# The second half's first LayerNorm, made on x passed in turned layout, with row statistics spread through DRAM

## The chip, the cores and the metric

The kernel runs on one core of one Trainium2 chip. Five engines work side by side, each executing its own queue in order: TensorE (PE, with its weight loads listed apart as PEld), VectorE (DVE), ScalarE (ACT), GpSimd (POOL) and SyncE (SP), which here only issues transfers; 16 DMA engines move the data. The metric is the device time of one execution in microseconds (us); less is better. A change of 0.2% is 3.5 us.

## The reference

One transformer block in float32, S = 2048 rows of width D = 512, with six modulation vectors from a condition c:

```python
mod = (_silu(c) @ w_mod).reshape(c.shape[0], 6, 1, -1)
sa, ca, ga, sb, cb, gb = (mod[:, 0], ..., mod[:, 5])
h = _layernorm(x, axis=-1) * (1 + ca) + sa
x = x + ga * attention(h)      # 32 query heads, 8 key/value heads, the last 512 keys
h = _layernorm(x, axis=-1) * (1 + cb) + sb
x = x + gb * ((gelu(h @ w_gate) * (h @ w_up)) @ w_down)
```

LayerNorm here is (x - mean) / sqrt(var + 1e-5) along a row. The change concerns the first LayerNorm, for rows 1024 to 2047 alone.

## The kernel before

**Numbers.** Float32 operands are split into two float16 parts, high and low, and every product is made of three float16 matmuls (`mm3`, line 83; the matmul's own line is 87). From group 3 on the projections use a seven-product scheme on 2 x 2 blocks, which needs sums and differences of blocks of h ("combos", t1 to t4).

**The main loop.** Attention is worked in 512 steps. A step t makes the scores of 128 query rows of one head against the 512 keys (`scores`, "ps", in one of two PSUM banks), then on VectorE the row maximum (`peak`, "nm", line 974), on ScalarE the exponential (`expo`, "ee", line 983), and two and three steps later the float16 parts of the probabilities (`high` on ScalarE, line 995; `low` on VectorE, line 1000). SP then turns these by a transposing transfer ("pt"). Four steps are a unit, one head on 512 query rows; 16 steps are a group (two heads, two row blocks). Steps 0 to 255 treat rows 0 to 1023, steps 256 to 511 rows 1024 to 2047; the first half's h is generation 0, the second half's generation 1. Between the scores TensorE works off a list, three items of three matmuls a step: projections ("qa", "qb", "qc"), probabilities times values ("po"), output projections ("py").

**Order.** All is written out by hand: each engine executes its instructions in the order in which the Python code issues them, step by step. Within a step the scores come first, then the maximum, `low`, the exponential, `high`, the list's items, the loads that are due, and last the work hung on the step as `("w", t)`. VectorE's work hung on step t therefore stands ahead of the maximum of step t + 1.

**Loads.** Float32 tiles go through the pool "raw" of five buffers. `sched(pos, (load, steps), ...)` names the steps at which a tile is used; a load is issued three steps ahead of its first use, or later where a slot, counted in rotation, is not free by the last use of the tile five loads earlier, but no later than the first use's step. SP issues in order, so a transfer that waits for an engine holds those behind it.

**GpSimd's other work** in each group of 16 steps, for the first half: the scale of the next weights (`w_spread`, one step ahead of the group, powers in tiles "lw", "lt"), the five parts of a weight set (`set_steps`, at 2, 3, 4, 6 and 8 steps into a group), a split of the keys at 9, of the values at 6 in every second, and four "wo" tiles for every second group (`parts`, line 640): at 6 and 4 steps before and 10 and 12 steps into it, but for the group of step 192 at 6, 4, 3 and 2 steps before it.

**The changed part.** `plan_gen(1, ...)` normalizes rows 1024 to 2047 ahead of time, in eight tiles of 128 rows, one every 16 steps from step 78 to step 190. For a tile first used at step t, `ln_tile` (lines 465 to 516) does: at t the statistics on VectorE (lines 378 to 382) and the power -1/2 on GpSimd (line 388); at t + 3 the norm on VectorE (line 486); at t + 5 four 128 x 128 float32 transposes on TensorE into a PSUM bank "pln" (line 491); at t + 6 and t + 7 the affine on ScalarE, four pieces of 128 x 128 (line 499), and a store of h to DRAM ("hs"); at t + 8 and t + 9 the high parts on ScalarE (line 511) and the low parts on GpSimd (line 513), for the blocks b11 and b21 (all columns of the first 512 rows) and b22 (the last 256 columns of the other 512). From step 201 on, and again from 234, `combos` reloads four columns' blocks from DRAM and makes t1 to t4 (lines 365, 369, 565). The same `ln_tile` serves a second LayerNorm elsewhere (generation 2), which stays.

Of the kernel before, what the change touches and what calls it, by code (L numbers as in the profile page):

```python
# [21 lines left out]
KT = D // P  # L22
NF = F // P
NT = S // P
QB = 512
QT = QB // P
EPS = 1e-5
# [31 lines left out]


@with_exitstack
def block_kernel(ctx: ExitStack, tc: tile.TileContext, x, kT, v, wq, wo, wg, wu, wd, cT, wc, wm, out):
    nc = tc.nc

    const = ctx.enter_context(tc.tile_pool(name="const", bufs=1))
    pool = ctx.enter_context(tc.tile_pool(name="pool", bufs=2))
    small = ctx.enter_context(tc.tile_pool(name="small", bufs=4))
    dram = ctx.enter_context(tc.tile_pool(name="dram", bufs=1, space=bass.MemoryType.DRAM))
# [5 lines left out]
    def raw(name):  # L74
        return pool.tile([P, 512], F32, tag="raw", name=name, bufs=NRAW)
# [4 lines left out]
    def bank(tag, name, bufs):  # L80
        return psum.tile([P, 512], F32, tag=tag, name=name, bufs=bufs)
# [9 lines left out]
    def dma(out_, in_):  # L91
        moved[0] += 1
        nc.sync.dma_start(out_, in_)
# [5 lines left out]
    def rows_of(t, i):  # L99
        return t[i * P:(i + 1) * P, :]  # L100
# [8 lines left out]
    nhalf = const.tile([P, 1], F32, name="nhalf")  # L109
# [19 lines left out]
    cols = const.tile([P, 6, KT], F32, name="cols")  # L129
# [105 lines left out]
    def pool_ts(out, src, a, b=1.0, op0=ALU.mult, op1=ALU.mult):  # L235
        nc.gpsimd.tensor_scalar(out, src, a, b, op0=op0, op1=op1)
# [136 lines left out]
    def ln_cols(key):  # L373
        return (1, 0) if key == "a" else (4, 3)

    def ln_stat(a, st, act=False):
        bn = small.tile([P, 6], F32, name="bn")
        nc.vector.bn_stats(bn, a)
        st["mv"] = small.tile([P, 2], F32, name="mv")
        nc.vector.bn_aggr(st["mv"], bn)  # L380
        st["rs"] = small.tile([P, 1], F32, name="rs")
        nc.vector.tensor_scalar(st["rs"], st["mv"][:, 1:2], EPS, None, op0=ALU.add)
        if act:
            st["nm"] = small.tile([P, 1], F32, name="nmean")
            nc.vector.tensor_scalar(st["nm"], st["mv"][:, 0:1], -1.0, None, op0=ALU.mult)

    def ln_power(st):
        nc.gpsimd.tensor_tensor(st["rs"], st["rs"], nhalf, op=ALU.pow)
# [78 lines left out]
    def ln_tile(gen, i, src):  # L467
        jsc, jsh = ln_cols("a" if gen < 2 else "f")
        qb, i = divmod(i % (2 * QT), QT)
        st = {}  # L470

        def load():
            if gen == 2:
                st["x"] = src()
            else:
                st["x"] = raw("xs")
                dma(st["x"], src())

        def stat():
            ln_stat(st["x"], st)  # L480
            ln_power(st)

        def norm():
            if gen == 2:
                return pool_ts(st["x"], st["x"], st["mv"][:, 0:1], st["rs"], ALU.subtract, ALU.mult)
            nc.vector.tensor_scalar(st["x"], st["x"], st["mv"][:, 0:1], st["rs"], op0=ALU.subtract, op1=ALU.mult)

        def turn():
            st["ps"] = bank("acc", "pln", NACC)
            for dt in range(KT):  # L490
                nc.tensor.transpose(st["ps"][:, dt * P:(dt + 1) * P], st["x"][:, dt * P:(dt + 1) * P], ident)

        def affine(dts):
            if 0 in dts:
                st["f"] = raw("hf") if gen == 2 else tmp("hf")
            f = st["f"]
            for dt in dts:
                sl = slice(dt * P, (dt + 1) * P)
                nc.scalar.activation(f[:, sl], st["ps"][:, sl], AF.Identity,
                                     scale=cols[:, jsc, dt:dt + 1], bias=cols[:, jsh, dt:dt + 1])  # L500
            if KT - 1 in dts:
                dma(spilled(gen, qb)[:, :, i * P:(i + 1) * P], f.rearrange("p (k q) -> p k q", k=KT))

        def parts(act):
            o = slice(i * P, (i + 1) * P)
            f = st["f"].rearrange("p (k q) -> p k q", k=KT)
            for h, name in enumerate(("b11", "b21") if qb == 0 else (None, "b22")):
                if name:
                    t, src = block(gen, name), f[:, 2 * h:2 * h + 2, :]
                    if act:  # L510
                        nc.scalar.activation(t[:, 0:2, o], src, AF.Copy)
                    else:
                        nc.gpsimd.tensor_tensor(t[:, 2:4, o], src, t[:, 0:2, o], op=ALU.subtract)

        more = [lambda: parts(True), lambda: parts(False)]
        return load, [stat, norm, turn, lambda: affine((0, 1)), lambda: affine((2, 3))] + more
# [82 lines left out]
    def sched(pos, ld, *more, kind="raw", ahead=AHEAD):  # L599
        loads.append(((pos,) + more, ld, kind, ahead))  # L600
# [121 lines left out]
    def at(key, *fns):  # L722
        later.setdefault(key, []).extend(fns)
# [442 lines left out]
    def sched_combos(gen, p, base):  # L1166
        for k, (load, steps) in enumerate(combos(gen, p, nc.gpsimd if gen or p == 0 else nc.vector, False, 0 if gen else 1 if p else 2, 0 if gen or p else 5)):
            if gen == 0 and (p == 0 or k > 1):
                at(base + ((0, 0, 0, 2)[k] if p else (-10, -2, -1, -9)[k]), load)
                for off, fn in steps:  # L1170
                    at(("w", base + off), fn)
            else:
                sched(base + steps[0][0], (load, [fn for _, fn in steps]), *[base + off for off, _ in steps[1:]])
# [1 line left out]
    for p in range(2):  # L1175
        sched_combos(0, p, CB[p])

    def plan_gen(gen, t_ln, t_cb, dcb, src):
        for i in range(2 * QT):
            t = t_ln[i]  # L1180
            load, steps = ln_tile(gen, i, lambda i=i: src(i))
            sched(t, (load, steps[:3]), t + 3, t + 5)
            for off, fn in zip((6, 7, 8, 9), steps[3:]):
                at(("w", t + off), fn)
        for p in range(2):
            sched_combos(gen, p, t_cb + dcb * p)

    plan_gen(1, [78 + 16 * i for i in range(8)], 201, 33, lambda i: rows_of(x, 2 * QT + i))
    for p in range(2):
        sched_combos(2, p, 478 + 10 * p)  # L1190

# [10 lines left out]
    for g in range(NG):  # L1202
        half, pr = divmod(g, NPR)
        t0 = 16 * g
# [404 lines left out]
    assert not later, list(later)  # L1609


_LAYOUT = ["x", "kT", "v", "wq", "wo", "wg", "wu", "wd", "cT", "wc", "wm"]


# [29 lines left out]
```

## Time and profile before

| what | value |
|---|---|
| median of 3 runs | 1746.63 us (1746.54 to 1746.77) |
| profiled execution, its time | 1747.24 us |
| its span | 1745.3 us |
| matmul busy, share of the span | 1723.9 us, 99% |
| VectorE, ScalarE, GpSimd busy | 79%, 70%, 52% |
| granted TensorE clock, mean | 1.00 |

The span is the part of the execution that the profile covers, from first to last instruction. A row of a timeline gives start and duration in us, engine, line, operation, output and inputs by the program's names, the shape and a count; in square brackets stands the idle time of the engine just before it and what ended that. A row of a group gives, under a tile's name, the least, median and largest duration in ns.

### The profile page before, as it was taken

To read this page: it belongs to the slowest core of one execution; us is meant where nothing else is said; L and a number is where in the kernel's file an instruction comes from. 1 tells how busy PE (TensorE), PEld (TensorE's weight loads), DVE (VectorE), ACT (ScalarE), POOL (GpSimd) and SP (SyncE) were. 2 spreads that over 40 slices of the span, in tenths; PEclk is the share of its full clock that TensorE was granted. 3 is DMA by queue.
4 is the path that set the end of the run, shared out by engine and by line. 5 is a ranking of instruction groups with operands and counts; after the bars stand their busy time and mean duration, and the time that the engine had idled before them with its cause. 6 is when DMAs were issued, how large, how long until landed. Compare 5 with 4: busy or idle time off the path is not lost.

```text
span 1745.3 us, 25819 instructions
## 1 busy us (share of the span) xinstructions
PE 1723.9 (99%) x8080; PEld 793.2 (45%) x8082; DVE 1380.3 (79%) x2404; ACT 1213.7 (70%) x2751; POOL 901.1 (52%) x1120
## 2 busy tenths in 40 slices
PE   7999999999999999999999999999999999999999
PEld 5444444444444444444444444444444444444444
DVE  7898898888889999888888888888886655555555
ACT  6988788888879777888777777877784544323232
POOL 4889778776788884654475565554521224000000
PEclk9999999999999999999999999999999999999999
DMA  7999999999999999999999999999986753252222
GB/s 234 219 206 211 211 215 206 225 209 219 213 219 228 212 205 183 212 208 235 212 201 215 203 220 199 211 214 213 195 184 145 205 174 117 81 183 77 88 75 76
DMA packets 667498, 329.71 MB, mean 189 GB/s; under 512 B 561504, under 2 KB 580192, under 8 KB 667360
## 3 DMA queue, kind: packets, MB, share of 16 engines
q1 hardware_dynamic: 667072, 327.54, 82.0%
q8 instruction: 64, 1.05, 0.3%
q14 instruction: 74, 0.61, 0.1%
q10 hardware_dynamic: 288, 0.52, 0.1%
HBM read 131.73 MB, written 59.90 MB: 110 GB/s over the span
## 4 chain that ended last, share of the span: by engine, by line
PE 87%; DVE 4%; ACT 4%; issue 1%; DMA 1%; POOL 1%; SPq 0%; ACTq 0%; POOLq 0%; DVEq 0%
PE py L87 25%; PE po L87 17%; PE ps L87 16%; PE fa L87 8%; PE qa L87 8%; PE fc L87 4%; PE qc L87 4%; PE qb L87 2%; PE fb L87 2%; ACT ee L983 1%; DVE p L1000 1%; ACT p L995 1%; DVE nm L974 1%; DMA pt<-p 1%; PE pq L87 1%
## 5 line engine op out<-in xcount | busy, mean ns | idle before, releaser
L983 ACT ACTIVATE ee<-ps,nm 128x512 f32<-128x512 f32 x512 | 350.2, 684 | 199.2 <-DVE nm L974 196.5
L1000 DVE SCALAR_TENSOR_TENSOR p<-ee,rr,p 128x512 f16<-128x512 f32 x512 | 460.7, 900 | 5.1 <-ACT p L995 4.7
L974 DVE TENSOR_REDUCE nm<-ps 128x1 f32<-128x512 f32 x512 | 350.3, 684 | 111.5 <-PE ps L87 108.4
L87 PE MATMUL ps<-k,qt 128*128 128x512 f16 x1536 | 414.9, 379 | 5.4 <-ACT ee L983 4.2
L87 PE MATMUL po<-pt,v 128*128 128x512 f16 x1536 | 373.0, 379 | 2.0 <-DMA pt<-p 2.0
L995 ACT ACTIVATE p<-ee,rr 128x512 f16<-128x512 f32 x512 | 364.4, 712 | 13.1 <-DVE rr L991 8.8
L87 PE MATMUL py<-wo,ot 128*128 128x512 f16 x1536 | 371.5, 379 | 0.0
L87 PEld LDWEIGHTS <-w 128*128 128x128 f16 x2184 | 213.5, 98 | 258.1 <-DVE w L1045 0.6
L87 PEld LDWEIGHTS <-v 128*128 128x128 f16 x1536 | 149.9, 98 | 184.3 <-DMA pt<-p 2.5
L87 PEld LDWEIGHTS <-ot 128*128 128x128 f16 x1536 | 150.2, 98 | 181.7 <-DVE ot L731 0.5
L87 PEld LDWEIGHTS <-qt 128*128 128x128 f16 x1536 | 145.9, 98 | 176.7 <-issue 4.3
L87 PE MATMUL py<-wo,at 128*128 128x512 f16 x672 | 160.5, 379 | 0.0
L943 DVE SCALAR_TENSOR_TENSOR acc<-py,dysc,acc 128x512 f32<-128x512 f32 x112 | 81.5, 747 | 51.1 <-PE py L87 51.1
L731 DVE SCALAR_TENSOR_TENSOR ot<-po,ot 128x512 f16<-128x512 f32 x128 | 87.7, 685 | 33.0 <-ACT ot L730 32.2
L87 PEld LDWEIGHTS <-at 128*128 128x128 f16 x672 | 65.7, 98 | 79.3
L983 ACT ACTIVATION_READ_ACCUMULATOR ee<-ps,nm 128x1 f32 x512 | 99.9, 195 | 0.0
L943 DVE SCALAR_TENSOR_TENSOR acc<-py,ysc,acc 128x512 f32<-128x512 f32 x128 | 94.7, 740 | 6.2 <-PE py L87 6.2
L1281 ACT ACTIVATE at<-fg 128x512 f16<-128x512 f32 x56 | 35.2, 628 | 72.2 <-DVE fg L1279 71.9
L87 PE MATMUL qa<-t,w 128*128 128x512 f16 x348 | 84.9, 379 | 0.0
L87 PE MATMUL fa<-t,w 128*128 128x512 f16 x336 | 82.0, 379 | 0.0
L730 ACT ACTIVATE ot<-po 128x512 f16<-128x512 f32 x128 | 73.9, 577 | 5.0 <-PE po L87 5.0
L232 POOL TENSOR_TENSOR lw<-lw,half__86 128x1 f32<-128x1 f32 x37 | 22.1, 598 | 104.6 <-DVE lw L182 104.5
(222 smaller groups left out, 2379.9 us busy)
## 6 DMA issues: line engine op xcount, KB each, us to landing
w<-kept SPq DMA_DIRECT2D x123, 256.0 KB, 3.2
wo<-kept SPq DMA_DIRECT2D x60, 256.0 KB, 3.8
raw<-in_wo SPq DMA_DIRECT2D x56, 256.0 KB, 3.3
kept<-stage SPq DMA_DIRECT2D x56, 256.0 KB, 3.4
kept<-w SPq DMA_DIRECT2D x39, 256.0 KB, 3.4
rw<-in_wq SPq DMA_DIRECT2D x38, 256.0 KB, 3.2
hs<-hf SPq DMA_DIRECT2D x32, 256.0 KB, 2.9
pt<-p SPq DMA_TRANSPOSE x512, 3.5
```

Source lines behind the costliest of these rows:

```text
L87: nc.tensor.matmul(ps, a, b, start=first and n == 0, stop=last and n == 2, skip_group_check=chain)
L232: nc.gpsimd.tensor_tensor(out, out, half_, op=ALU.pow)
L730: nc.scalar.activation(t[:, 0, :], src, AF.Copy, scale=scale)
L731: return lambda: nc.vector.scalar_tensor_tensor(t[:, 1, :], src, scale, t[:, 0, :], op0=ALU.mult, op1=ALU.subtract)
L943: nc.vector.scalar_tensor_tensor(acc[ti], st["p"], by, acc[ti], op0=ALU.mult, op1=ALU.add)
L974: nc.vector.tensor_reduce(nm, E[t]["ps"], axis=AX.X, op=ALU.max, negate=True)
L983: nc.scalar.activation(e, E[t]["ps"], AF.Exp, bias=E[t]["nm"], scale=1.0, accum_out=sm[:, t % 2:t % 2 + 1])
L995: nc.scalar.activation(p16[:, 0, :], E[t]["e"], AF.Copy, scale=E[t]["r"])
L1000: nc.vector.scalar_tensor_tensor(p16[:, 1, :], E[t]["e"], E[t]["r"], p16[:, 0, :], op0=ALU.mult, op1=ALU.subtract)
L1281: nc.scalar.activation(t[:, 0, :], g, AF.Copy)
```

## The change

The host passes a second copy of the last 1024 rows of x, turned: `xT`, ordered as two blocks of 512 rows, four blocks of 128 columns, with the columns on partitions. `plan_turned(78)` replaces `plan_gen(1, ...)`.

- `stat_rows`: eight row tiles of x, one every 8 steps from step 78 to 134, are loaded only for their statistics. Mean and variance are made as before; the mean and, by GpSimd's power, the inverse root are put into a small tile, four row tiles side by side.
- `spread_stats`: that tile (128 partitions x 8 values) is written to DRAM in the order (kind, row tile, row), four bytes apiece, at steps 106 and 138.
- `fetch_stats`: at steps 139 and 171 the 1024 values are read back to all 128 partitions, 4 KB each, into one buffer.
- `x_turned`: eight turned tiles (128 columns x 512 rows), one every 8 steps from t = 144 to 200. At t GpSimd subtracts the mean, at t + 1 VectorE multiplies by the inverse root, at t + 2 ScalarE does the affine with one column's scale and shift per partition, at t + 4 SP stores h and ScalarE makes the high part, at t + 5 GpSimd makes the low part, the latter two for six of the eight tiles.
- No transposes are made for this LayerNorm, and no PSUM bank is used by it. The combinations keep their steps.
- The scratch for descriptors made in software is set to 1024 bytes.

```diff
+    def stat_rows(qb, i):
...
+            bn = small.tile([P, 6], F32, name="bn")
+            nc.vector.bn_stats(bn, st["x"])
+            mv = small.tile([P, 2], F32, name="mv")
+            nc.vector.bn_aggr(mv, bn)
+            s = SB["s", qb]
+            nc.vector.tensor_scalar(s[:, 1, i:i + 1], mv[:, 1:2], EPS, None, op0=ALU.add)
+            nc.gpsimd.tensor_scalar(s[:, 0, i:i + 1], mv[:, 0:1], 1.0, 1.0, op0=ALU.mult, op1=ALU.mult)
+            nc.gpsimd.tensor_tensor(s[:, 1, i:i + 1], s[:, 1, i:i + 1], nhalf, op=ALU.pow)
...
+    def spread_stats(qb):
+        SB["d", qb] = dram.tile([2, QT, P], F32, name=f"xsd{qb}")
+        dma(SB["d", qb].rearrange("k i p -> p k i"), SB["s", qb])
+
+    def fetch_stats(qb):
+        SB[qb] = pool.tile([P, 2, QB], F32, tag="xsb", name="xsb", bufs=1)
+        dma(SB[qb].rearrange("p k r -> p (k r)"), SB["d", qb].rearrange("k i p -> (k i p)").partition_broadcast(P))
+
+    def x_turned(qb, dt):
...
+        def load():
+            st["x"] = raw("xt")
+            dma(st["x"], xT[qb, dt])
+        def centre():
+            nc.gpsimd.tensor_tensor(st["x"], st["x"], SB[qb][:, 0, :], op=ALU.subtract)
+        def scale():
+            nc.vector.tensor_tensor(st["x"], st["x"], SB[qb][:, 1, :], op=ALU.mult)
+        def affine():
+            nc.scalar.activation(st["x"], st["x"], AF.Identity, scale=cols[:, 1, dt:dt + 1], bias=cols[:, 0, dt:dt + 1])
+        def keep_():
+            dma(spilled(1, qb)[:, dt, :], st["x"])
+            if name:
+                nc.scalar.activation(block(1, name)[:, p, :], st["x"], AF.Copy)
+        def low():
+            if name:
+                t = block(1, name)
+                nc.gpsimd.tensor_tensor(t[:, 2 + p, :], st["x"], t[:, p, :], op=ALU.subtract)
...
+    def plan_turned(t0):
+        for j in range(8):
+            qb, i = divmod(j, QT)
+            load, stat = stat_rows(qb, i)
+            sched(t0 + 8 * j, (load, [stat]))
+            if i == QT - 1:
+                at(("w", t0 + 8 * j + 4), lambda qb=qb: spread_stats(qb))
+        for j in range(8):
+            qb, dt = divmod(j, KT)
+            t = t0 + 66 + 8 * j
+            load, steps = x_turned(qb, dt)
+            sched(t, (load, steps), t + 1, t + 2, t + 4, t + 5)
+            if dt == 0:
+                at(("w", t - 5), lambda qb=qb: fetch_stats(qb))
...
-    plan_gen(1, [78 + 16 * i for i in range(8)], 201, 33, lambda i: rows_of(x, 2 * QT + i))
+            sched_combos(1, p, 201 + 33 * p)
+
+    plan_turned(78)
```

More of the change, by code (lines that the diff above doesn't have):

```diff
@@ L61, in block_kernel @@
 @with_exitstack
-def block_kernel(ctx: ExitStack, tc: tile.TileContext, x, kT, v, wq, wo, wg, wu, wd, cT, wc, wm, out):
+def block_kernel(ctx: ExitStack, tc: tile.TileContext, x, xT, kT, v, wq, wo, wg, wu, wd, cT, wc, wm, out):
     nc = tc.nc
@@ L1176, in block_kernel, with stat @@
         sched_combos(0, p, CB[p])
[L1178 to L1184, printed above, removed]
+    SB = {}
+    def stat_rows(qb, i):
+        st = {}
+        def load():
+            st["x"] = raw("xs")
+            dma(st["x"], rows_of(x, (2 + qb) * QT + i))
+        def stat():
+            if i == 0:
+                SB["s", qb] = small.tile([P, 2, QT], F32, tag="xst", name="xst", bufs=2)
+            bn = small.tile([P, 6], F32, name="bn")
[6 more added lines that the diff above has]
+            nc.gpsimd.tensor_tensor(s[:, 1, i:i + 1], s[:, 1, i:i + 1], nhalf, op=ALU.pow)
+        return load, stat
@@ new lines, in spread_stats, with load @@
+    def spread_stats(qb):
[5 more added lines that the diff above has]
+    def x_turned(qb, dt):
+        st = {}
+        name = (("b11", "b21"), (None, "b22"))[qb][dt // 2]
+        p = dt % 2
+        def load():
+            st["x"] = raw("xt")
[14 more added lines that the diff above has]
+                nc.gpsimd.tensor_tensor(t[:, 2 + p, :], st["x"], t[:, p, :], op=ALU.subtract)
+        return load, [centre, scale, affine, keep_, low]
@@ L1185, in plan_gen @@
         for p in range(2):
-            sched_combos(gen, p, t_cb + dcb * p)
-    plan_gen(1, [78 + 16 * i for i in range(8)], 201, 33, lambda i: rows_of(x, 2 * QT + i))
+            sched_combos(1, p, 201 + 33 * p)
+    plan_turned(78)
     for p in range(2):
@@ L1609, in block_kernel @@
     assert not later, list(later)
-_LAYOUT = ["x", "kT", "v", "wq", "wo", "wg", "wu", "wd", "cT", "wc", "wm"]
+_LAYOUT = ["x", "xT", "kT", "v", "wq", "wo", "wg", "wu", "wd", "cT", "wc", "wm"]
 def kernel(A_x, A_k_cache, A_v_cache, A_wq, A_wo, B_x, B_w_gate, B_w_up, B_w_down, c, w_mod):
@@ L1623 @@
         "x": a["x"][0],
+        "xT": a["x"][0, 2 * QB:].T.reshape(KT, P, 2, QB).transpose(2, 0, 1, 3),
         "kT": a["k"][0, :, sk - W:, :].transpose(0, 2, 1),
@@ L1635 @@
     ins = {k: np.ascontiguousarray(t) for k, t in ins.items()}
-    nc = _bacc.Bacc("TRN2", target_bir_lowering=False, num_devices=1)
+    nc = _bacc.Bacc("TRN2", target_bir_lowering=False, num_devices=1, dynamic_dma_scratch_size=1024)
     args = [nc.dram_tensor(f"in_{k}", ins[k].shape, mybir.dt.from_np(ins[k].dtype), kind="ExternalInput").ap()
```

## The prediction

> **What bounds the kernel now.** I read the page's busy shares and its chain first, then busy time by stretch, then the instructions in order of time where the changed rows are now treated.
>
> ```profile
> span 1745.3 us, 25819 instructions
> PE 1723.9 (99%) x8080; PEld 793.2 (45%) x8082; DVE 1380.3 (79%) x2404; ACT 1213.7 (70%) x2751; POOL 901.1 (52%) x1120
> PE 87%; DVE 4%; ACT 4%; issue 1%; DMA 1%; POOL 1%; SPq 0%; ACTq 0%; POOLq 0%; DVEq 0%
> ```
> ```profile
> 500.00:600.00 100.00, 99.40 (x468) 45.26 (x467) 88.55 (x152) 83.25 (x202) 86.36 (x103) 1.00 1.01 219
> ```
> TensorE is busy 99% of the span at full clock, and the chain is mostly its own. So work taken from it comes back in full, and a wait put into it costs in full. In the stretch, whose columns are PE, PEld, DVE, ACT, POOL, clock and DMA share, VectorE and GpSimd have only some 12% to spare, and GpSimd is the one that the change loads.
>
> **What leaves TensorE.** Columns below: start, duration.
>
> ```profile
> 438.00 0.60 PE L491 MATMUL pln<-ident,xs 128*128 128x128 f32 x4
> 438.44 0.17 PE L219 MATMUL pst<-lm,ones 128*128 128x1 bf16 x1
> L491 PE MATMUL pln<-ident,xs x32: 272/273/273, 234.8 to 519.6; 128*128 128x128 f32 x32
> ```
> The four transposes of a tile hold the stream from 438.00 to 438.44, not 4 x 273 ns, since they overlap: 0.44 us. Eight tiles: **-3.5 us**. Their waits on other engines were nil in this stretch.
>
> **What the other engines gain and lose.**
>
> ```profile
> L499 ACT ACTIVATE hf<-pln,cols x64: 438/452/483, 239.3 to 781.1; 128x128 f32<-128x128 f32 x64
> L511 ACT ACTIVATE b<-hf x24: 399/414/433, 244.5 to 786.7; 128x256 f16<-128x256 f32 x24
> L513 POOL TENSOR_TENSOR b<-hf,b x24: 663/672/1121, 245.7 to 789.8; 128x256 f16<-128x256 f32 x24
> L530 ACT ACTIVATE xs<-xs,kinv,kmax x8: 798/812/814, 1363.7 to 1399.8; 128x512 f32<-128x512 f32 x8
> L486 DVE TENSOR_SCALAR xs<-xs,mv,rs x8: 532/541/546, 230.7 to 517.3; 128x512 f32<-128x512 f32 x8
> L565 POOL TENSOR_TENSOR cb<-cb x27: 1262/1272/1727, 99.9 to 1470.3; 128x512 f32<-128x512 f32 x27
> L365 ACT ACTIVATE t<-cb x28: 612/620/631, 75.7 to 1471.6; 128x512 f16<-128x512 f32 x28
> L369 POOL TENSOR_TENSOR t<-cb,t x25: 1149/1159/1698, 94.6 to 1472.7; 128x512 f16<-128x512 f32 x25
> ```
> ScalarE: 32 x 0.45 + 12 x 0.41 = 19.3 us go, 8 x 0.81 + 6 x 0.62 = 10.2 us come. A gain of 9 us off the path, taken as nothing. VectorE: eight norms of 0.54 go, eight scalings of two SBUF operands come. No row has that form; the nearest are the norm (0.54) and the PSUM sum in a fence below (0.68), so 0.65, about 1 us more in all, hidden in the 12%; at most 1 us if not. GpSimd: 12 x 0.67 = 8 us go, 8 x 1.27 (subtracting the mean) + 6 x 1.16 (low parts) = 17.2 us come, and eight tiny products (0.2 us each, like its other one-column steps). Nine to eleven us more, and not spread evenly.
>
> SP: 16 loads for 8, still 8 stores, and four transfers of statistics: 12 more issues of about 0.57 us in some 330 us. The transfers:
>
> ```profile
> q1 hardware_dynamic: 667072, 327.54, 82.0%
> pt<-p SPq DMA_TRANSPOSE x512, 3.5
> cb<-hs SPq DMA_DIRECT2D x28, 256.0 KB, 4.7
> 540.17 6.66 DMA pt<-p
> 547.08 2.10 PE L87 MATMUL po<-pt,v 128*128 128x512 f16 x9 [0.60 <-DMA pt<-p]
> ```
> Two of the new transfers write 1,024 four-byte pieces each, two read 512 KB each. All 667,072 packets take 82% of 16 engines' span, 34 ns of one engine each, so 1,024 pieces cost 16 engines 2.2 us (estimate). Issues fall behind the last transpose of a score unit and before a first one, which has three more steps. The one late transpose of this stretch landed after 6.66 us, 3.2 above the median, and cost TensorE 0.60. Bounds for the two scatters: 0 and 2 x 0.6; I take 0. The stores in 2 KB rows instead of 512 B rows go the other way. SP also waits in order: for GpSimd's power before each scatter (four steps, some 10 us, later), and before the second fetch for tile 3's scaling (two steps later); transposes queue behind both, and I charge nothing, with the same 0.6 each as the other end. The smaller descriptor scratch touches no queue that the page lists: nothing. The Trainium skill, "DMA: Bandwidth & Descriptors", section Rules for kernel authors, says that a non-contiguous last dimension makes one descriptor per element, and under Specifications that below 512 B a write is read-modify-write; no run here shows such pieces, and by that rule the upper bound, 1.2 us, would be the likelier.
>
> **The wait that the change adds.** In program order GpSimd subtracts the mean at step t, VectorE scales at t+1, ScalarE applies the affine at t+2, with t = 144, 152, ... 200 for turned tiles 0 to 7. VectorE executes in order: if GpSimd is late, the row maxima, the exponentials and two steps on the next scores queue behind the scaling, because "ps" has two banks. Before, VectorE's norm waited for GpSimd's power with three steps between, and that failed once, at the last old tile (power in step 190, norm in 193):
>
> ```profile
> DVE xs L486 <- POOL rs L388: 2.3, 1, 2.3
> ```
> ```profile
> 517.30 0.55 DVE L486 TENSOR_SCALAR xs<-xs,mv,rs 128x512 f32<-128x512 f32 x1 [2.29 <-POOL rs L388]
> 517.76 0.68 DVE L974 TENSOR_REDUCE nm<-ps 128x1 f32<-128x512 f32 x1
> ...
> 518.48 0.69 ACT L983 ACTIVATE ee<-ps,nm 128x512 f32<-128x512 f32 x1 [1.28 <-DVE nm L974]
> 519.75 0.81 PE L87 MATMUL ps<-k,qt 128*128 128x512 f16 x3
> ```
> This is the price list. GpSimd ended at 517.26, the exponential at 519.1: 1.85 us later, 1.95 with a scaling of 0.65. The scores that reuse the bank began at 519.75: the 2.29 us were absorbed with 0.6 to spare. So a tile costs TensorE (end of subtraction + 1.95) minus the time its scores two steps on are due. Now GpSimd around these steps:
>
> ```profile
> 512.53 1.81 POOL L640 TENSOR_TENSOR raw<-raw,gs 128x512 f32<-128x512 f32 x1
> 516.69 0.57 POOL L388 TENSOR_TENSOR rs<-rs,nhalf 128x1 f32<-128x1 f32 x1
> 517.23 0.65 POOL L232 TENSOR_TENSOR lw<-lw,half__86 128x1 f32<-128x1 f32 x1
> 519.33 0.60 POOL L236 TENSOR_SCALAR lt<-lt 128x1 f32<-128x1 f32 x1
> ...
> 538.30 1.16 POOL L156 TENSOR_TENSOR w<-rw,w 128x512 f16<-128x512 f32 x1
> ```
> Tile 6 (step 192, scaled in 193). GpSimd is late from the four "wo" tiles of steps 186 to 190 (the last is the L640 at 512.53). Behind it comes the weight scale of step 191, from 517.23 to 519.93; without the power 0.54 earlier, 519.4. Then the subtraction, to 520.7. Scores due at 519.75 - 0.43 (a turn gone) = 519.3, possible at 522.65: **+3.3 us**. VectorE would wait from 515.0 to 520.7. The load of that "wo" tile moves from step 187 to 190, because the slot rule counts turned tile 5 until 189; at step 190 SP issued at 509.47 (row below), and 3.3 us of landing gives 512.8 for a start at 512.53, so 0.3, not counted.
>
> ```profile
> 509.47 0.50 SPq L93 DMA_DIRECT2D raw<-in_v  x1
> 535.91 0.68 DVE L754 TENSOR_TENSOR qc<-u,qc 128x512 f32<-128x512 f32 x1
> 540.47 0.81 PE L87 MATMUL ps<-k,qt 128*128 128x512 f16 x3
> ```
> Tile 7 (200, scaled in 201, after that L754). GpSimd does the set's last parts until 539.46. It shifts by 3.45 (its next step waits for VectorE's reciprocal, which is behind tile 6's scaling) and by 1.16 - 0.67 for other low parts; plus 1.27, it ends at 544.7. Scores possible at 546.65, due at 540.47 + 2.9 = 543.35: **+3.3**.
>
> ```profile
> 453.95 0.68 DVE L754 TENSOR_TENSOR qc<-u,qc 128x512 f32<-128x512 f32 x1
> 455.23 1.15 POOL L156 TENSOR_TENSOR w<-rw,w 128x512 f16<-128x512 f32 x1
> 459.18 0.81 PE L87 MATMUL ps<-k,qt 128*128 128x512 f16 x3
> 412.52 1.48 POOL L156 TENSOR_TENSOR w<-rw,w 128x512 f16<-128x512 f32 x1
> 418.55 0.81 PE L87 MATMUL ps<-k,qt 128*128 128x512 f16 x3
> 431.45 0.58 POOL L236 TENSOR_SCALAR lt<-lt 128x1 f32<-128x1 f32 x1
> 433.64 0.54 DVE L486 TENSOR_SCALAR xs<-xs,mv,rs 128x512 f32<-128x512 f32 x1
> ```
> Tile 3 (168): the same parts end at 456.4, the subtraction at 457.8 with 0.1 of moved low parts; VectorE was ready at 454.6. Possible 459.75, due 459.18 - 0.43: **+1.0**. Tile 1 (152): 414.0 + 1.3 + 1.95 = 417.25, due 418.1: absorbed, nothing; tile 5 stands at the same place of the pattern and is taken alike. Tile 2: GpSimd is free at 432.0, done at 433.3, VectorE comes at 433.64: no wait; tiles 0 and 4 follow the same short steps. After tiles 3, 6 and 7 VectorE stays late and repeats part of the miss one step on: 0.5 in all, an estimate from the 0.6 us margin.
>
> **The sum.** -3.5 + 3.3 + 3.3 + 1.0 + 0.5 = +4.6 us. Made against the profiled execution (1747.24 us, span 1745.3) it gives 1751.8; the median shown is 0.6 below that execution, so 1751.2 us, 0.26% slower.
>
> A rule bears on the scaling. GpSimd's tensor rows above stretch beside other work, from 1262 to 1727 ns (L565) and from 663 to 1121 ns (L513). The Trainium skill, "SBUF — State Buffer", section Who interferes with whom, says that a VectorE instruction with two SBUF inputs and a GpSimd instruction that reads SBUF block each other for a whole instruction. The stretched rows agree with it. By that rule the three late scalings could each be held by the next GpSimd step for 0.7 to 1.3 us, and the sum would be +7 to +8; by the rows above it stays at +4.6.
>
> **The rivals.**
> (a) The waits are absorbed and only the 3.5 us remain: 1743.1, faster. Place: tiles 6 and 7. It needs the subtraction of tile 6 to end by 519.3 - 1.95 = 517.35, 3.3 us before my figure. For it: 2.29 us were absorbed already, and GpSimd would have to reach the subtraction without the weight scale ahead of it. Against: in its order of time from the L640 at 512.53 to the part at 538.30 GpSimd has no idle entry, so nothing gives way.
> (b) Only one of the two late places charges TensorE, because a delay there lets GpSimd catch up before the other: 1751.2 - 3.3 = 1747.9, no change. For: TensorE's pause gives everyone time. Against: GpSimd's next step itself waits for VectorE, so it shifts along.
> (c) The lateness goes on into the combinations of step 203: "b22" is loaded at 203 instead of 200 by the slot rule, and 4.7 us of landing hold GpSimd, whose weight scale VectorE needs at step 210. A second wait like tile 6's, or locked scalings: +3 to +6, 1754 to 1757.
> (d) The statistics' scatters delay transposes: +0.6 each beside (a), 1744.3.
>
> **How the numbers follow.** My case 0.54, (b) 0.20, (c) 0.13, (a) 0.10, (d) 0.03. The range leaves out (a) and (d) below and ends above (c): 1745 to 1758; my case's own range is 1749 to 1754. A change of 0.2% (3.5 us) is about what can be told from none. Slower than 1750.1: most of my case and (c), 0.63. Faster than 1743.1: (a)'s edge, 0.10. Between: 0.27.
>
> **What would show it.** Right: no "pln" from "xs"; VectorE waits on GpSimd's subtraction for 5 us or so at two scalings near 515 to 545 us, and less at one near 455; TensorE idle before "ps" for the exponential, 3 us each, in the same places. Wrong: GpSimd reaching tile 6 without wait; the idle time standing before "po" for a transfer; or VectorE's waits there with TensorE still at 100%.

## The result: 1.3% slower, and the profile after

The changed kernel takes 1770.06 us (median of 4 runs, 1769.29 to 1771.29) against 1746.7 us for the kernel before: a ratio of 1.0131, 95% interval 1.0113 to 1.0148. It is 23.4 us slower, where the forecast was 4.6 and the range ended at 1758. The direction was right; the size was not, and half of the loss has a cause that the forecast put at nothing.

The head and the chain on the page of the changed kernel; the share of VectorE, ScalarE and GpSimd in the chain has grown from 9% to 17%:

```profile
span 1767.5 us, 25749 instructions
PE 1730.5 (98%) x8048; PEld 790.7 (45%) x8050; DVE 1377.8 (78%) x2404; ACT 1209.2 (68%) x2721; POOL 914.3 (52%) x1130
PE 78%; DVE 7%; ACT 6%; POOL 4%; issue 2%; DMA 2%; SPq 0%; ACTq 0%; POOLq 0%; DVEq 0%
```

Busy time by stretch of the changed kernel (columns PE, PEld, DVE, ACT, POOL, granted clock, DMA share, GB/s). The stretch from 500 to 600 answers the one shown of before:

```profile
300.00:400.00 100.00, 92.55 (x426) 41.21 (x425) 79.03 (x149) 72.51 (x175) 69.33 (x96) 0.97 1.01 192
400.00:500.00 100.00, 96.19 (x436) 42.57 (x435) 81.73 (x147) 81.30 (x192) 78.77 (x96) 0.98 1.01 225
500.00:600.00 100.00, 93.57 (x421) 41.21 (x420) 80.11 (x140) 76.45 (x178) 83.31 (x102) 0.97 0.93 211
```

TensorE is idle for 7.5, 3.8 and 6.4 us in the three stretches behind 300 us (before: 0.0, 0.0 and 0.6), and the granted clock is below 1.00 in the same three (before: 1.00). The forecast had places between 455 and 545 us only; two fifths of the idle time stand earlier, between 300 and 400 us. The longest kinds of waits between 225 and 600 us (who waits for whom: total, times, longest, in us):

```profile
PE ps L87 <- ACT ee L983: 13.2, 8, 4.0
DVE xt L1222 <- POOL xt L1219: 17.0, 6, 5.2
DVE bn L1191 <- DMA xs<-in_x: 5.5, 1, 5.5
DVE p L1000 <- ACT p L995: 6.4, 6, 4.3
```

VectorE waits 17.0 us for GpSimd's subtraction, as was said; the last two rows are waits that the forecast didn't have. To see what each place cost TensorE, the start of every "ps" is compared with the start of the same scores in the trace of before. The difference between the two traces steps up where time is lost:

| place | forecast | measured |
|---|---|---|
| eight turns gone, 0.44 each | -3.5 | -3.5 |
| first scatter, 310 us | 0 | +5.8 |
| second scatter, 390 us | 0 | +6.4 |
| turned tile 1 (waits of "ps" and "qa", each under 0.4) | 0 | +1.4 |
| turned tile 3 | +1.0 | +3.5 |
| turned tile 5 | 0 | +0.8 |
| turned tile 6 | +3.3 | +7.6 |
| turned tile 7 | +3.3 | +1.6 |
| repeats | +0.5 | in the rows above |
| sum | +4.6 | +23.6 |

The sum is that of the stretch from 225 to 600 us; outside it the two traces differ by 1.4 us the other way, so that their whole spans are 22.2 us apart. The two halves are about equal: 12.2 us around the scatters of the statistics, 14.9 us at the turned tiles.

**The first scatter.** From the changed kernel's timeline, in order of time, rows of SP, VectorE and TensorE (start and duration in us, engine, operation; in brackets the idle time before it and what ended that); the last row is from the kernel before, the "qa" of the same step:

```profile
296.10 0.43 SPq L93 DMA_DIRECT2D xsd<-xst  x1
301.74 7.97 SPq L1004 DMA_TRANSPOSE pt<-p  x1
309.82 0.69 DVE L1191 BATCH_NORM_STATS2 bn<-xs 128x6 f32<-128x512 f32 x1 [5.49 <-DMA xs<-in_x]
312.38 1.44 PE L87 MATMUL ps<-k,qt 128*128 128x512 f16 x3 [3.62 <-ACT ee L983]
314.19 2.25 PE L87 MATMUL qa<-t,x 128*128 128x512 f16 x6 [0.38 <-ACT u L876]
316.28 0.81 PE L87 MATMUL py<-wo,ot 128*128 128x512 f16 x3
```
```profile
310.25 1.46 PE L87 MATMUL qa<-t,x 128*128 128x512 f16 x6
```
```profile
xsd<-xst SPq DMA_DIRECT2D x2, 4.0 KB, 9.6
```

Above, the scatters among the changed kernel's transfers (how many, size, median us from issue to landing); below, its busy time in two stretches of 10 us, with the columns as before, and then the first of the two in the kernel before:

```profile
300.00:310.00 10.00, 8.75 (x43) 3.87 (x42) 4.17 (x8) 4.42 (x12) 5.21 (x6) 1.00 0.79 50
310.00:320.00 10.00, 7.24 (x27) 2.88 (x27) 7.80 (x20) 8.39 (x22) 3.06 (x8) 0.83 1.10 264
```
```profile
300.00:310.00 10.00, 10.00 (x50) 4.53 (x48) 8.83 (x18) 8.31 (x23) 8.52 (x12) 1.00 1.06 221
```

The 4 KB took 9.6 us to land (median of the two scatters). Meanwhile the 16 engines were 79% busy but moved 50 GB/s, where the kernel before moved 221. The row tile of x loaded behind it came late, VectorE waited 5.49 us for it in front of the row maximum of the next scores, and SP took 7.97 us over a transpose that usually takes it 1.23. The trace also times each packet. The 1,024 pieces took 9 ns each, and all were begun between 297.9 and 298.7 us. What stood behind them was slow: from 299.5 to 309 us packets of 256 B took 110 ns on average and up to 4.9 us (24 on average in the kernel before), packets of 2 KB 485 ns (107). So the pieces themselves were cheap; dear was that they held up what came after them. TensorE lost 3.62 + 0.38 us to waits. The remaining 1.6 us came afterwards: the granted clock was 0.83, the three matmuls of "ps" took 1.44 us instead of 0.81 and the six of "qa" 2.25 instead of 1.46, and the next starts moved by 0.78 and 0.79 us.

The second scatter went another way to the same end. No load of statistics stood behind it. SP took 8.55 us over a transpose, the buffers of the probabilities weren't freed, and "high" (ScalarE) and with it "low" (VectorE) came late:

```profile
387.94 8.55 SPq L1004 DMA_TRANSPOSE pt<-p  x1
394.63 0.72 ACT L995 ACTIVATE p<-ee,rr 128x512 f16<-128x512 f32 x1 [4.74 <-DMA pt<-p]
396.07 0.81 PE L87 MATMUL ps<-k,qt 128*128 128x512 f16 x3 [1.16 <-ACT ee L983]
399.17 2.72 PE L87 MATMUL qa<-t,x 128*128 128x512 f16 x6 [2.29 <-ACT u L876]
```

**Turned tile 6**, from the timeline of the changed kernel, GpSimd first, then VectorE and TensorE:

```profile
529.43 1.45 POOL L640 TENSOR_TENSOR raw<-raw,gs 128x512 f32<-128x512 f32 x1 [2.81 <-DMA raw<-in_wo]
535.34 1.26 POOL L1219 TENSOR_TENSOR xt<-xt,xsb 128x512 f32<-128x512 f32 x1
536.64 0.69 DVE L1222 TENSOR_TENSOR xt<-xt,xsb 128x512 f32<-128x512 f32 x1 [5.20 <-POOL xt L1219]
538.79 1.44 PE L87 MATMUL ps<-k,qt 128*128 128x512 f16 x3 [3.95 <-ACT ee L983]
540.03 2.77 PE L87 MATMUL qc<-t,w 128*128 128x512 f16 x6
542.59 1.49 PE L87 MATMUL py<-wo,ot 128*128 128x512 f16 x3
543.87 1.14 PE L87 MATMUL ps<-k,qt 128*128 128x512 f16 x3
```

This is the chain that the prediction wrote down: GpSimd late from the "wo" tiles, the subtraction, 5.20 us of waiting on VectorE (5.7 were forecast), the exponential, "ps". TensorE's wait of 3.95 us is near the forecast 3.3. What wasn't forecast is the 2.81 us that GpSimd waited for a "wo" load, and the clock behind TensorE's wait. From 538.79 on four items start 1.24, 2.56, 1.28 and 0.97 us apart instead of 0.65, 1.30, 0.65 and 0.65: 2.8 us more. The last 0.7 us was lost at a wait of "qa" for ScalarE, at 528.85 us.

### The profile page after: what moved, and what is told of

It is laid out like the page before. It is cut to its first block, busy times and chain, and to the rows that moved or that the text cites. A ratio compares the mean times of both kernels' runs of the same rounds, so it can differ in the third digit from the quotient of the medians.

```text
span 1767.5 us, 25749 instructions
## 1 busy us (share of the span) xinstructions
PE 1730.5 (98%) x8048; PEld 790.7 (45%) x8050; DVE 1377.8 (78%) x2404; ACT 1209.2 (68%) x2721; POOL 914.3 (52%) x1130
## 4 chain that ended last, share of the span: by engine, by line
PE 78%; DVE 7%; ACT 6%; POOL 4%; issue 2%; DMA 2%; SPq 0%; ACTq 0%; POOLq 0%; DVEq 0%
PE py L87 23%; PE ps L87 14%; PE po L87 14%; PE fa L87 8%; PE qa L87 7%; PE fc L87 4%; PE qc L87 3%; PE fb L87 2%; ACT ee L983 2%; PE qb L87 2%; DVE p L1000 2%; DVE nm L974 2%; ACT p L995 2%; DVE qt L731 1%; PE pq L87 1%
## 5 line engine op out<-in xcount | busy, mean ns | idle before, releaser
L1000 DVE SCALAR_TENSOR_TENSOR p<-ee,rr,p 128x512 f16<-128x512 f32 x512 | 459.4, 897 | 10.2 <-ACT p L995 9.7
```

Source lines behind the costliest of these rows:

```text
L1000: nc.vector.scalar_tensor_tensor(p16[:, 1, :], E[t]["e"], E[t]["r"], p16[:, 0, :], op0=ALU.mult, op1=ALU.subtract)
```

## The experiments

The median times of the kernel before, in the runs that each experiment is compared with, were between 1747.0 and 1747.2 us. "Tiles' term" below is what TensorE lost at the turned tiles, found as in the table (14.9 in the changed kernel). It is read from one traced execution, which lay up to 2.5 us above the median.

**1. The scatters alone.** Added to the kernel before, at the same two steps and with the change's own pattern:

```diff
+    def scatter(n):
+        d = dram.tile([2, QT, P], F32, name=f"xsd{n}")
+        dma(d.rearrange("k i p -> p k i"), ident[:, 0:2 * QT].rearrange("p (k i) -> p k i", k=2))
+    for n, t in enumerate((106, 138)):
+        at(("w", t), lambda n=n: scatter(n))
```

> The kernel before, unchanged but for two transfers of 1,024 four-byte pieces each, written to DRAM from a constant tile at steps 106 and 138; nobody reads them. Theory A (a scatter keeps the transfer rings busy for some 8 us, and what queues behind it starves VectorE, ScalarE and then TensorE): the same jumps as in the changed kernel, +5.7 and +6.4 us, so 1746.7 + 12 = 1758.8 us. Rival (the rings are full because of the added loads of x and of the broadcast read, the scatter is only in the wrong place): 1746.5 to 1748 us.

Measured: 1764.01 us, ratio 1.0094 (1.0077 to 1.0111). The landing, from its transfers, and then the same chain as above, from its timeline:

```profile
xsd<-ident SPq DMA_DIRECT2D x2, 4.0 KB, 12.1
```
```profile
313.84 0.69 DVE L378 BATCH_NORM_STATS2 bn<-xs 128x6 f32<-128x512 f32 x1 [7.47 <-DMA xs<-in_x]
316.39 1.44 PE L87 MATMUL ps<-k,qt 128*128 128x512 f16 x3 [5.44 <-ACT ee L983]
```

Two stores of 4 KB, with nothing else changed, cost 17 us by the medians; in the trace they cost 7.5 and 8.7 at their two places. That is theory A's cause, and 5 us more than its figure. At the second place a row tile that VectorE waits for (6.46 us) now stands behind the scatter. Why the first place also cost more than in the changed kernel, with 12.4 us to land instead of 9.9, isn't shown.

**2. The same bytes in a quarter of the pieces.** In the changed kernel:

```diff
-        SB["d", qb] = dram.tile([2, QT, P], F32, name=f"xsd{qb}")
-        dma(SB["d", qb].rearrange("k i p -> p k i"), SB["s", qb])
+        SB["d", qb] = dram.tile([2, P, QT], F32, name=f"xsd{qb}")
+        dma(SB["d", qb].rearrange("k p i -> p k i"), SB["s", qb])
...
-        dma(SB[qb].rearrange("p k r -> p (k r)"), SB["d", qb].rearrange("k i p -> (k i p)").partition_broadcast(P))
+        dma(SB[qb].rearrange("p k r -> p (k r)"), SB["d", qb].rearrange("k p i -> (k p i)").partition_broadcast(P))
```

The read takes the values in that order, so rows get one another's statistics in this run.

> The changed kernel with the same statistics written in 256 pieces of 16 bytes, row by row, instead of 1,024 of 4 bytes; they come back in another order, so the output is not the reference's, and all else is as in the changed kernel. Theory A, price by the piece: a landing of 2.5 to 4.5 us instead of 9.6 and nearly no wait there, 1770.1 - 12 = 1758 us. Rival (price by bytes or by the transfer, or the broadcast read): 1768 to 1771 us. If it were all the scatter's, the late subtractions too, 1744 to 1747 us.

Measured: 1759.91 us, ratio 1.0072 (1.0057 to 1.0087). Its transfers, and its waits between 225 and 600 us:

```profile
xsd<-xst SPq DMA_DIRECT2D x2, 4.0 KB, 4.1
```
```profile
PE ps L87 <- ACT ee L983: 10.0, 7, 3.9
```

256 pieces of 16 B landed in 4.1 us and cost TensorE nothing; 10.2 us of the loss are gone. What is left is the tiles' term, 15.2 us.

**3. What is it about the pieces?** Four stores of other shapes in the kernel before, at steps 74, 106, 138 and 170 (the comments are added here):

```diff
+    def half_as_many():      # 512 pieces of 4 B, neighbours
+        d = dram.tile([QT, P], F32, name="da")
+        dma(d.rearrange("i p -> p i"), ident[:, 0:QT])
+    def far_apart():         # 1,024 pieces of 4 B, 64 B apart
+        d = dram.tile([2, QT, P, 16], F32, name="db")
+        dma(d[:, :, :, 0].rearrange("k i p -> p k i"), ident[:, 0:2 * QT].rearrange("p (k i) -> p k i", k=2))
+    def longer():            # 1,024 pieces of 64 B
+        d = dram.tile([2, QT, P, 16], F32, name="dc")
+        dma(d.rearrange("k i p e -> p (k i) e"), ident.rearrange("p (k e) -> p k e", e=16))
+    def whole():             # 128 pieces of 32 B
+        d = dram.tile([P, 2 * QT], F32, name="dd")
+        dma(d, ident[:, 0:2 * QT])
```

> The kernel before with four transfers to DRAM that nobody reads, 32 steps apart: 512 pieces of 4 bytes side by side (step 74), 1,024 of 4 bytes each 64 bytes from the next (106), 1,024 of 64 bytes (138), 128 of 32 bytes (170). Price by the piece: landings of some 5 to 6, 9.6, 9.6 and 2.5 us. Rival, neighbours in one line that several rings write get in each other's way: 5 to 6, 3 to 4, 3 to 4 and 2.5 us.

Measured: 1754.58 us in a single run. Its transfers (size, median us to landing):

```profile
dc<-ident SPq DMA_DIRECT2D x1, 64.0 KB, 4.1
da<-ident SPq DMA_DIRECT2D x1, 2.0 KB, 10.6
db<-ident SPq DMA_DIRECT2D x1, 4.0 KB, 5.7
dd<-ident SPq DMA_DIRECT2D x1, 4.0 KB, 2.7
```

Only "da" cost anything (7.3 us). Twice as many four-byte pieces, but 64 B apart, landed in 5.7 us and were hidden; as many pieces of 64 B landed in 4.1. So neither the number of pieces nor their four bytes set the price alone, and neither does lying side by side: the pieces of 64 B and the 16 B pieces of experiment 2 also lay next to pieces from other partitions, and landed in 4.1 us. Dear were pieces that were both, four bytes long and side by side. That such small neighbouring writes hold one another up fits this; by what mechanism, and up to which size or distance, no run here shows. The price by the piece is refuted. The rival came near for the pieces of 64 and 32 B, but it had 3 to 4 us for those 64 B apart and 5 to 6 for the 512.

**4. The scaling first.** In the changed kernel VectorE scales at t, and GpSimd subtracts mean times root, with three steps until the affine:

```diff
-            nc.gpsimd.tensor_scalar(s[:, 0, i:i + 1], mv[:, 0:1], 1.0, 1.0, op0=ALU.mult, op1=ALU.mult)
             nc.gpsimd.tensor_tensor(s[:, 1, i:i + 1], s[:, 1, i:i + 1], nhalf, op=ALU.pow)
+            nc.gpsimd.tensor_scalar(s[:, 0, i:i + 1], mv[:, 0:1], s[:, 1, i:i + 1], 1.0, op0=ALU.mult, op1=ALU.mult)
...
-        return load, [centre, scale, affine, keep_, low]
+        return load, [scale, centre, affine, keep_, low]
...
-            sched(t, (load, steps), t + 1, t + 2, t + 4, t + 5)
+            sched(t, (load, steps), t, t + 3, t + 4, t + 5)
```

> The changed kernel, with VectorE's scaling made first (at step t) and GpSimd's subtraction, of mean times inverse root, behind it; ScalarE's affine moves from t + 2 to t + 3. VectorE no longer waits for GpSimd; scatters stay. Theory B (GpSimd's lateness at the turned tiles costs 1.4 + 3.5 + 0.8 + 5.0 + 1.6 = 12.3 us): 1770.1 - 12.3 = 1757.8 us. Rival (the wait goes on to ScalarE, which needs the subtraction one to two steps later): 1764 to 1771 us. Rival (all is the scatter's): 1769 to 1771 us.

Measured: 1770.06 us, ratio 1.0131 (1.0116 to 1.0146): no gain at all. VectorE's wait for GpSimd is gone and the tiles' term fell from 14.9 to 8.7, but the scatters cost 18.1 instead of 12.2. Behind the first one SP took 11.22 us over the transpose instead of 7.97, with the same transfers in between; why, isn't shown. A new wait of TensorE came up as well (between 225 and 600 us):

```profile
PE po L87 <- POOL v L156: 3.8, 2, 2.7
```

GpSimd is as late as before; now the values' split ("v") is what it brings too late. The next four runs take the scatters out, so that this can be seen by itself.

**5 to 8. No scatter; then the subtraction in four places.** In all four, TensorE turns the statistics, at 0.11 us for each half, and eight rows of 512 B are stored:

```diff
+        ps = bank("acc", "pst", NACC)
+        nc.tensor.transpose(ps[0:2 * QT, 0:P], SB["s", qb].rearrange("p k i -> p (k i)"), ident)
+        t = small.tile([2 * QT, P], F32, tag="xtt", name="xtt", bufs=2)
+        nc.scalar.activation(t, ps[0:2 * QT, 0:P], AF.Copy)
-        dma(SB["d", qb].rearrange("k i p -> p k i"), SB["s", qb])
+        dma(SB["d", qb].rearrange("k i p -> (k i) p"), t)
```

With nothing else changed:

> The changed kernel, only with the statistics turned by TensorE and stored in rows of 512 B, all else in the change's own order: the same result as the changed kernel, without a scatter. Theory A: the two jumps at the scatters (5.7 and 6.4 us) go, the tiles' waits stay at 12 to 15 us: 1756 to 1760 us, and TensorE's waits stand at tiles 1, 3, 6 and 7 only. Theory B (the scatters' delays had caused part of the later lateness, and the run with longer pieces, whose statistics stood in the wrong rows, isn't a fair copy): under 1752.

With the scaling first, as in 4:

> The changed kernel, with the statistics turned by TensorE and stored in rows (no scatter), and VectorE's scaling put first, at its load's step, so that it doesn't wait for GpSimd; GpSimd then subtracts mean times root. Theory A (GpSimd itself has 10 us too much to do between step 144 and 216, so the lateness shows at its next reader): -3.5 + 0.6 + about 8.7, as in the run with the scaling first but without its two scatter jumps: 1751 to 1753 us. Theory B (the wait is only a matter of who stands first, and the scatters disturbed the run with the scaling first): 1744 to 1746.

With `nc.vector.tensor_tensor` for the subtraction in `centre`:

> The changed kernel, with two edits: the statistics are turned by one TensorE transpose per half and stored as 8 rows of 512 B instead of 1,024 pieces of 4 B, and VectorE makes the subtraction of the mean as well as the scaling, so that GpSimd loses 8 x 1.26 = 10 us and VectorE gains 8 x 0.69 = 5.5 us. Theory A (the loss is the scatters, 12 us, and the scaling's wait on GpSimd, another 12): both are gone, the 3.5 us of the old turns stay gone, the two new turns cost up to 0.3 each: 1743.5 to 1745 us against 1747.0 before, with VectorE's waits on GpSimd for these tiles at zero. Theory B (VectorE, with 12% to spare in this stretch, becomes the bound once it does both): row maxima and exponentials come late by 0.7 us at each of eight tiles, 1748 to 1751.

With `centre` empty:

> The changed kernel, with the statistics turned by TensorE and stored in rows (no scatter), and without the subtraction of the mean, which is left out altogether (the rows are only scaled, so this LayerNorm isn't centred). GpSimd is 10 us lighter, VectorE unchanged. Theory A (the subtraction's 1.26 us in front of each scaling is the whole second cause): 1743.5 to 1745 us. Theory B (the low parts, which grew from 8 to 7 us in other places, or the second load per tile are part of it): some of the waits of tiles 3 and 6 stay, 1747 to 1753.

| run | time, us | ratio, 95% interval | tiles' term |
|---|---|---|---|
| turn alone | 1759.56 | 1.0068 (1.0055 to 1.0082) | 16.4 |
| scaling first | 1753.69 | 1.0033 (1.0022 to 1.0043) | 9.1 |
| both on VectorE | 1749.02 | 1.0013 (1.0004 to 1.0022) | 6.4 |
| no subtraction | 1746.87 | 0.9998 (0.9988 to 1.0007) | 2.6 |

Theory A held for the first run and nearly for the second, so the scatters' delays hadn't caused the tiles' waits. It was too hopeful for the last two. Without the subtraction the time lies between the two theories' ranges, 0.1 us under theory B's. With both on VectorE the time is theory B's, but not its mechanism: TensorE waited 2.7 us for GpSimd's split of the values and 0.8 for exponentials. The waits of these runs between 225 and 600 us, one fence a run, in the order of the table:

```profile
PE ps L87 <- ACT ee L983: 10.7, 8, 4.0
DVE xt L1226 <- POOL xt L1223: 19.5, 6, 5.2
```
```profile
PE po L87 <- POOL v L156: 3.8, 2, 2.7
```
```profile
PE po L87 <- POOL v L156: 2.7, 2, 2.0
PE ps L87 <- ACT ee L983: 0.8, 2, 0.6
```
```profile
PE ps L87 <- ACT ee L983: 1.1, 1, 1.1
```

The subtraction on GpSimd, ahead of VectorE, costs 1759.56 - 1746.87 = 12.7 us; on VectorE it costs 2.2. Even without any subtraction only 0.3 of the 3.3 us remain that the turns saved net: some 3 us are lost in other ways, which were not taken apart. In the traced execution 2.6 us are lost at the tiles, in waits for GpSimd's splits and for one exponential. With both on VectorE one scaling of eight also took 1.64 us where the others took 0.68; it ran beside a GpSimd split of 1.72 us:

```profile
514.61 1.41 POOL L640 TENSOR_TENSOR raw<-raw,gs 128x512 f32<-128x512 f32 x1 [2.85 <-DMA raw<-in_wo]
517.13 1.72 POOL L156 TENSOR_TENSOR wo<-raw,wo 128x512 f16<-128x512 f32 x1
517.76 1.64 DVE L1226 TENSOR_TENSOR xt<-xt,xsb 128x512 f32<-128x512 f32 x1
```

**9 to 12. Slot or place?** That run's wait of 2.85 us for a "wo" load, which a turned tile's slot had put off, led to two edits: the five parts in steps t, t, t + 1, t + 2, t + 3 (`sched(t, (load, steps), t, t + 1, t + 2, t + 3)`), and the whole plan 16 steps earlier (`plan_turned(62)`).

> The run with both operations on VectorE, with one more edit: a turned tile goes through its five parts in steps t, t+1, t+2, t+3 and not t, t+1, t+2, t+4, t+5, so that it gives its load slot back two steps (5 us) sooner. In the run with both on VectorE the fourth wo tile's load came 8.7 us later than before, GpSimd waited 2.85 us for it, and TensorE lost 5 us between 505 and 550 us. Theory A (the slot that turned tile 5 holds is what makes GpSimd late there): the wait of 2.85 us goes, 1745 to 1747 us. Theory B (it is GpSimd's low parts, 1.16 to 1.65 us at these steps): no change, 1749.

> The run with both operations on VectorE, with the whole plan of this LayerNorm 16 steps (some 41 us) earlier: statistics from step 62, turned tiles from step 128 to 184, so that none of them meets the four wo tiles of steps 186 to 190 or the set's last parts behind them. Theory A (the loss is of the place, where GpSimd is busiest): only the 3.5 us of the turns and 0.6 for the two new ones remain, 1743.5 to 1745 us. Theory B (GpSimd's added work costs wherever it stands): 1748 to 1750.

> The run with TensorE turning the statistics and the change's own order (GpSimd subtracts, VectorE scales one step later), with the whole plan 16 steps earlier, as above. Theory A (place): the waits of tiles 6 and 7, some 7 to 8 us of its 13 to 15, go; those at the places of tiles 1 and 3, two steps of the pattern that come again every 16, stay: 1750 to 1754 us. Theory B (GpSimd ahead of VectorE costs at every tile, wherever it stands): 1757 to 1760.

> Both operations on VectorE, the shorter hold and the plan 16 steps earlier, in one kernel. If the two edits reach the same loss, it is as fast as the better one of them, 1743.5 to 1745 us; if they reach different parts and each gains alone, it is faster than both; theory B of both: 1748 to 1750.

| run | time, us | ratio, 95% interval |
|---|---|---|
| both on VectorE, shorter hold | 1751.49 | 1.0027 (1.0017 to 1.0037) |
| both on VectorE, earlier | 1749.23 | 1.0011 (1.0002 to 1.0021) |
| turn alone, earlier | 1754.41 | 1.0041 (1.0027 to 1.0055) |
| both on VectorE, shorter hold and earlier | 1747.72 | 1.0004 (0.9995 to 1.0012) |

The shorter hold took the wait for the "wo" load away, and the kernel became no faster; its median is 2.5 us higher, with intervals that overlap. So neither theory held, and in the kernel with both on VectorE the slot wasn't the cause. What that load costs where GpSimd subtracts, this run doesn't say. The earlier place gave 5 us where GpSimd still subtracts ahead of VectorE (1759.56 to 1754.41), 0.4 above theory A's range, and nothing where VectorE does both (1749.02 to 1749.23), as theory B said. The best version, with no scatter, both operations on VectorE, shorter and earlier, is within the measurement of the kernel before. Its median is 1.5 us under that of the earlier plan alone and 3.8 under that of the shorter hold alone, though neither had gained by itself; no expectation had this, and no run takes it apart. No version beat it.

## Why the prediction was wrong, point by point

**"Bounds for the two scatters: 0 and 2 x 0.6; I take 0."** This step failed, and it is half of the miss: 12.2 us measured. The working priced pieces by the average packet, 34 ns, and got 2.2 us of 16 engines for 1,024 of them. The pieces took less, 9 ns each; what the working put at nothing is that they hold up the packets behind them. The measured landing was 9.6 us in the changed kernel and 12.1 alone. The upper end was no bound either: it came from one late transpose that was hidden but for 0.60 us, and said nothing on a transfer that stops its queue for 8 us. The rule cited there, from the Trainium skill, "DMA: Bandwidth & Descriptors", section Rules for kernel authors, that a non-contiguous last dimension makes one descriptor per element, pointed the right way, though not to the size. The trace agrees with it: the scatter shows as 1,024 packets of 4 B. The runs add that such pieces were cheap when 64 B apart (5.7 us, hidden) and dear when side by side.

**The wait at the scaling: right in mechanism, mis-sized.** Tiles 6, 3, 7, 1, 5 cost 7.6, 3.5, 1.6, 1.4 and 0.8 where 3.3, 1.0, 3.3, 0 and 0 (and 0.5 of repeats) were forecast: 14.9 for 8.1. At tile 6 the wait came out near (3.95 for 3.3), but that is in part luck. The load of the last "wo" tile, put at 0.3 and "not counted", held GpSimd for 2.81 us, and from there to the end of the subtraction (529.43 to 536.60 us) GpSimd was never idle. Without that wait the subtraction could have ended up to 2.8 us sooner, and TensorE's pause would have been some 1.2 us (an estimate from these rows; no run takes this wait alone out while GpSimd subtracts). The term also left out the granted clock, which fell behind the pause and cost 2.8 us. The prediction's 1.95 us from the end of the subtraction to the scores was read a little short: its rows give 1.91 where it has 1.85, so 2.0, and 2.2 were measured here. At tile 3 GpSimd came 1.4 us later than worked out. A third of that arose in the last 9 us ahead of the subtraction, where the low part now took 1.64 us; the rest was lateness brought along from the steps before, which the working started at zero:

```profile
459.96 1.64 POOL L1235 TENSOR_TENSOR b<-xt,b 128x512 f16<-128x512 f32 x1
470.03 0.69 DVE L1222 TENSOR_TENSOR xt<-xt,xsb 128x512 f32<-128x512 f32 x1 [4.19 <-POOL xt L1219]
472.19 0.81 PE L87 MATMUL ps<-k,qt 128*128 128x512 f16 x3 [1.76 <-ACT ee L983]
476.12 0.81 PE L87 MATMUL ps<-k,qt 128*128 128x512 f16 x3 [1.18 <-ACT ee L983]
```

The wait repeats one step of the pattern on (1.76, then 1.18), so the 0.5 for all repeats was too little. At tile 7 the reasoning of rival (b) was right in part: TensorE's long pause at tile 6 let GpSimd catch up, and 1.6 of 3.3 us were charged. (That is some 2.3 us lost, less the 0.76 that a late transpose had cost the kernel before at this place.)

**The rest of the sum.** The -3.5 us of the turns came exactly, 0.44 us at each of eight places. Prices were right: subtraction 1.26 (1.27), scaling 0.69 (0.65), affine 0.80 (0.81), low parts 1.15 with some of 1.7. The fetch of the statistics cost nothing that shows in the table.

**The rivals.** (a), everything absorbed, fell: even without the subtraction 3 us of loss remained. (c), lateness going on into the combinations, came as far as GpSimd, which waited 5.4 us for a combination's load at 570 us, but TensorE lost under 0.7 us there. A late GpSimd held TensorE elsewhere, at the values' split, when the scaling stood first. (d), scatters delaying transposes, was the true one in kind, at 0.03, and ten times its price; it stood beside (a), which fell. The blocking between VectorE and GpSimd, for which the prediction had +7 to +8, didn't come at the scalings; in the changed kernel none was stretched:

```profile
L1222 DVE TENSOR_TENSOR xt<-xt,xsb x8: 678/693/694, 402.4 to 560.4; 128x512 f32<-128x512 f32 x8
```

In the run with both on VectorE one of eight was stretched (the 1.64 us above), beside a GpSimd instruction, which fits such blocking. Whether the stretched low part at tile 3 is such a case isn't shown.

The median times stack up as: 1770.06, less 10.5 for the scatters (turn alone), less 10.5 for moving the subtraction to VectorE, less 2.2 for leaving it out, is 1746.87. That is 3 us above the 1743.9 that the kernel before gives less 3.5 and plus 0.2 for the two new turns. These last 3 us were not taken apart.

## What to carry to other kernels

Before a store with a transposed pattern is called free, ask where its neighbouring elements come from: a few KB of four-byte pieces from many partitions, side by side in DRAM, can stop a queue for 8 us, and every transpose and load behind it. Turn such a tile on chip first; here that cost TensorE 0.11 us for each tile. Where an in-order engine with little to spare is put in front of another, in a kernel whose bound engine is 99% busy, start its lateness from what it already carries, count the loads that it waits for, and don't put its work one step ahead of its reader. And to each wait of the bound engine add what its clock does afterwards.

## What the runs showed of the hardware

**The clock falls behind a pause of some us.** Behind the pauses of 3.62 us (first scatter) and 3.95 us (tile 6) in the changed kernel, and behind the pair of 1.16 and 2.29 us at the second scatter, matmuls took nearly twice as long for 3 to 6 us; 1.6, 2.8 and 2.6 us were lost by it, 7 of the 23 in all. It also happened behind shorter single ones: 2.68 us in the run with turned statistics and the scaling first, and 2.00 us with both on VectorE.

```profile
544.61 0.82 PE L87 MATMUL po<-pt,v 128*128 128x512 f16 x3 [2.68 <-POOL v L156]
546.40 3.31 PE L87 MATMUL po<-pt,v 128*128 128x512 f16 x9
```
```profile
540.89 0.82 PE L87 MATMUL po<-pt,v 128*128 128x512 f16 x3 [2.00 <-POOL v L156]
542.20 3.79 PE L87 MATMUL po<-pt,v 128*128 128x512 f16 x9
```

Nine such matmuls usually take 2.1 us. Pauses of 1.76 and 1.18 us, 4 us apart, left the pace unchanged (the rows of tile 3). The Trainium skill, "TensorE: Matmul & The Clock Gate", Part 1, states that the clock goes to half after an idle window of about 3.4 us. The halved pace agrees; the pauses of 2.00 and 2.68 us, and the pair, are shorter than that window, and no run here shows why they sufficed.

**Neighbouring four-byte writes.** 512 of them took longer to land (10.6 us) than 1,024 that were 64 B apart (5.7 us) or 1,024 of 64 B (4.1 us), although these move 32 times the bytes.
